# Decoding of int64-packed weights: the low words' product on ScalarE and GpSimd, with four decoding steps a unit throughout

## The chip, the cores and the metric

The kernel runs on one core of a Trainium2 chip. The core's engines work in parallel, each with a queue of its own that it goes through in order: TensorE (PE; its weight loads are shown as PEld), VectorE (DVE), ScalarE (ACT), GpSimd (POOL) and SyncE (SP), which here issues DMAs. The metric is device time in microseconds (us) of one execution; a verdict compares medians of runs on the same chip.

## The reference

Block-sparse attention over q, k and v of shape (4, 8, 768, 64), followed by a gated projection. A query block of 32 rows sees the first and the last block, its neighbours, and three drawn blocks; the first and the last query block see everything. Cut to what matters:

```python
mask = np.abs(blk_i - blk_j) <= 1
mask = mask | (blk_i == 0) | (blk_j == 0) | (blk_i == n_blocks - 1) | (blk_j == n_blocks - 1)
for qb in range(n_blocks):
    for kb in sampled_blocks[qb]:
        mask[qb * block:(qb + 1) * block, kb * block:(kb + 1) * block] = True
scores = np.where(mask, scale * np.matmul(q, k.transpose(0, 1, 3, 2)), -1e9)
attn = np.exp(scores - max); attn = attn / (sum + 1e-09)
x = (attn @ v) as (B, S, H * D)                  # 4 x 768 x 512
gate_pre = sum over k < 5 of conv_w[k] * xp[:, k:k + S]   # causal convolution
gate = 1.0 / (1.0 + np.exp(-gate_pre))
out = (gate * (x @ w_val) @ w_out)               # w_val, w_out: 512 x 512
```

The three weight arrays reach the program as float64, seen as pairs of 32-bit words: the kernel has to make float32 values of them itself.

## The kernel before

Attention goes in *units*. Each batch has eleven pairs of query blocks, one unit each, and one pair of global blocks (first and last), which takes two units: 13 units a batch, 52 in all. A main loop over steps `n` (line 684) writes the program so that each step holds, for TensorE, the scores of unit n (`sc`, or `s` for a global one), the product with the values of unit n - 2 (`av`) and the transposes of unit n - 1 (`pt`). Around that, VectorE reduces the scores to their maximum (`mx`, two instructions for a pair), then divides `av` of unit n - 2 by its sum (`rs`, `x`), which TensorE transposes (`xp`) into `xT`. ScalarE makes the exponentials (`pe`), copies the transposed probabilities to SBUF (`ptr`), `xp` to `xT`, and scales queries (`qc`). GpSimd gathers value rows (`vb`, two indirect DMAs a unit, line 343) and copies key blocks into a tile that unit n + 2 will use (`kg`, five copies, line 308). Each step's gather needs the `vb` buffer that `av` of three units earlier has read. SP loads queries, keys, end and own value rows (`va`), and weights.

The order on each engine is the order in which the program is written: `InOrder` (line 71) ties each instruction to the one before it on its engine. What belongs to no unit is dealt out in small portions, `prepare(steps)` (line 646), called twice in the step of a pair, behind each half of the transposes (line 732). A portion is one `yield` of a generator. While weights are not all decoded, a portion is a step of `decode_weights` (line 204), which runs up to two tiles in turn; afterwards it is a step of the gates' convolution (`th`, on VectorE and ScalarE). `STEPS, MORE` (line 53) give two steps a call, and three in the units listed in `MORE`.

`decode(hi, lo, raw, n)` (line 154) turns a tile of 128 x 512 float64 values into two float32 parts: `hi`, the value rounded to float32r, and `lo`, the rest. `raw` is a staging tile (`wst`) of word pairs; `hw` is the high word and `lw` the low word of each, so consecutive elements of one of them lie 8 bytes apart. `t` (`words`) is scratch. Before the change a tile takes eight steps with VectorE instructions in seven of them alone and in the eighth with ScalarE's cast of `hi`. It is called for eight tiles, four of `w_val` (into `wv0`, `wv1`) and four of `w_out` (into `wo0`, `wo1`), and for the convolution's 20 columns (`cst` into `cwp`, then `cw`). The first portions run in step 2. There are four staging tiles, so the load of a `w_out` tile on SP (line 184) waits until the `w_val` tile in the same buffer is decoded. When all are decoded, the gates start, and later the projections (`vp`, `op`) of `project` (line 548), on TensorE between the parts of the units.

Of the kernel before, what the change touches and what calls it, by code (L numbers as in the profile page):

```python
# [7 lines left out]
F32 = mybir.dt.float32  # L8
# [3 lines left out]
AF = mybir.ActivationFunctionType  # L12
ALU = mybir.AluOpType
# [36 lines left out]
    {0: POOL, 1: POOL, 2: POOL, 3: DVE, 4: ACT},  # L50
] + [{0: POOL, 1: POOL, 2: POOL}] * (B - 2)

STEPS, MORE = 2, (*range(2, 7), *range(48, 53))

HELD = ()

# [2 lines left out]
def attention_moe(ctx, tc, qb, kb, v, sampled, w_val, conv_w, w_out, ident_in, slot_in, out):  # L59
# [29 lines left out]
    pe, dve, act, pool, sp = (InOrder(e) for e in (nc.tensor, nc.vector, nc.scalar, nc.gpsimd, nc.sync))  # L89
# [42 lines left out]
    for r in range(NR):  # L132
# [3 lines left out]
            out=base[rows, :], in0=sf[rows, r, :], scalar1=float(BLK), scalar2=off[rows], op0=ALU.mult, op1=ALU.add  # L136
# [17 lines left out]
    def decode(hi, lo, raw, n):  # L154

        hw, lw = raw[:, :, 1], raw[:, :, 0]
        t = two.tile([128, DM], F32, tag="ot", name="words").bitcast(I32)[:, 0:n]
        dve.tensor_scalar(out=t, in0=hw, scalar1=0x1FF, scalar2=15, op0=ALU.bitwise_and, op1=ALU.logical_shift_left)
        yield True
        dve.scalar_tensor_tensor(  # L160
            out=lw.bitcast(U32), in0=lw.bitcast(U32), scalar=17, in1=t.bitcast(U32),
            op0=ALU.logical_shift_right, op1=ALU.bitwise_or,
        )
        yield True

        dve.tensor_scalar(out=t, in0=hw, scalar1=0x7FFFFFFF, scalar2=None, op0=ALU.bitwise_and)
        yield True
        dve.tensor_scalar(
            out=t.bitcast(F32), in0=t.bitcast(F32), scalar1=2.0**-15, scalar2=2.0**16, op0=ALU.max, op1=ALU.mult
        )  # L170
        yield True
        dve.tensor_scalar(out=t, in0=t, scalar1=3, scalar2=0x7FFFF000, op0=ALU.logical_shift_left, op1=ALU.bitwise_and)
        yield True
        dve.scalar_tensor_tensor(out=t, in0=hw, scalar=-(1 << 31), in1=t, op0=ALU.bitwise_and, op1=ALU.bitwise_or)
        yield True
        dve.tensor_scalar(out=hw, in0=t, scalar1=-(1 << 23), scalar2=None, op0=ALU.bitwise_and)
        yield True
        dve.scalar_tensor_tensor(out=lo, in0=lw, scalar=2.0**-35, in1=hw.bitcast(F32), op0=ALU.mult, op1=ALU.mult)
        act.copy(hi, t.bitcast(F32))
        yield True  # L180

# [14 lines left out]
    def decode_conv():  # L196
        yield from decode(cwp[:, 0, :], cwp[:, 1, :], cst, CH * KW)
        dve.tensor_tensor(
            out=cw.rearrange("p c k -> p (c k)"), in0=cwp[:, 0, :].bitcast(F32), in1=cwp[:, 1, :].bitcast(F32),
            op=ALU.add,  # L200
        )
        yield True

    def decode_weights():

        jobs, begun = [(-1, decode_conv())], 0
        while step[0] < DECODE_LAG:
            yield False
        while jobs or begun < 2 * CH:
            n = begun  # L210
            if len(jobs) < 2 and n < 2 * CH and len(staged) > n and step[0] >= staged[n][0] + DECODE_LAG:
                dst = wv if n < CH else wo
                jobs.append((n, decode(dst[0][:, n % CH, :], dst[1][:, n % CH, :], staged[n][1], DM)))
                begun += 1
            if not jobs:
                yield False
                continue
            n, job = jobs.pop(0)
            if next(job, None):
                jobs.append((n, job))  # L220
                yield True
            else:
                decoded.add(n)
        decoded.add("all")
# [580 lines left out]
```

## Time and profile before

| | us |
|---|---|
| three runs | 398.83, 401.76, 400.08; median 400.08 |
| profiled execution | 400.6 |
| its span, first to last instruction | 398.8 |

| engine | busy us | share of the span |
|---|---|---|
| PE | 349.5 | 88% |
| PEld | 271.4 | 68% |
| DVE | 284.3 | 71% |
| ACT | 251.7 | 63% |
| POOL | 237.9 | 60% |

In the trace a row names the engine, the operation, the tile that is written and those that are read (`words<-wst`), the shape, a count, the busy time, and in square brackets the idle time in front of it with what ended it. Stretches of the same operation are merged into one row with their count. All instructions have line 77, the helper's line, so they are told apart by their tiles. A share over the whole span mixes stages: weights are decoded from 24 to 104 us, gates run from 103 us on, and projections from 130 us on.

### The profile page before, as it was taken

The numbers are of one execution on the slowest core, as the hardware profiler recorded it, in microseconds if no ns is written. First come the engines' busy times: TensorE is split into PE (matmuls) and PEld (weight loads), VectorE is DVE, ScalarE is ACT, GpSimd is POOL, SyncE is SP. The second block draws the span as 40 slices with busy tenths as digits, with TensorE's granted clock in tenths as the row PEclk, the third lists the DMA queues.
The fourth block names the chain that finished last, engine by engine and source line by source line (L and its number), as shares of the span: only waits on it lengthen the run. The fifth ranks groups of instructions, "written<-read, shape, count | busy, mean of one in ns | idle before, by whom it ended". The sixth has DMA issues, their size and how long they took to land.

```text
span 398.8 us, 16126 instructions
## 1 busy us (share of the span) xinstructions
PE 349.5 (88%) x6616; PEld 271.4 (68%) x6616; DVE 284.3 (71%) x595; ACT 251.7 (63%) x610; POOL 237.9 (60%) x377
## 2 busy tenths in 40 slices
PE   7697777787686999899789988998999999999896
PEld 5364455565464887697568866776678788789694
DVE  4478999995889679677937783776495746957820
ACT  1487787883897776665555764666576565754521
POOL 1836887495599667726671777367537765522730
PEclk9999999998999999989999999999999999999999
DMA  7968897888756756874253557564633254120102
GB/s 246 329 190 254 286 300 231 227 241 255 226 165 201 225 160 171 257 213 138 55 181 105 148 167 214 160 206 134 201 109 103 62 149 109 53 79 26 54 26 80
DMA packets 41305, 67.15 MB, mean 168 GB/s; under 512 B 5648, under 2 KB 21904, under 8 KB 41232
## 3 DMA queue, kind: packets, MB, share of 16 engines
q1 hardware_dynamic: 34048, 42.67, 34.7%
q0 software_dynamic: 7040, 23.43, 20.9%
q8 instruction: 52, 0.85, 0.8%
q14 instruction: 21, 0.17, 0.1%
q10 hardware_dynamic: 144, 0.03, 0.1%
HBM read 59.81 MB, written 6.29 MB: 166 GB/s over the span
## 4 chain that ended last, share of the span: by engine, by line
PE 57%; DVE 19%; DMA 8%; ACT 7%; issue 6%; another core or an unknown queue 1%; POOL 1%; SPq 1%; ACTq 0%; DVEq 0%
PE op L77 15%; PE vp L77 14%; PE av L77 10%; PE pt L77 8%; PE sc L77 7%; DVE mx L77 7%; DVE words L77 4%; DMA va<-in_v 3%; DMA wst<-in_w_val 3%; DVE wst L77 2%; DVE th L77 2%; PE xp L77 2%; DMA k<-in_k 2%; PE s L77 1%; ACT ptr L77 1%
## 5 line engine op out<-in xcount | busy, mean ns | idle before, releaser
L77 POOL DMA_INDIRECT vb<-in_v,idx x88 | 89.2, 1013 | 56.6 <-PE av L77 29.6
L77 ACT ACTIVATE pe<-sc,mx 128x256 f32<-128x256 f32 x176 | 69.2, 477 | 63.4 <-DVE mx L77 59.8
L77 DVE SCALAR_TENSOR_TENSOR th<-xT,cw,th 128x384 f32<-128x384 f32 x128 | 97.8, 767 | 6.4 <-ACT th L77 3.6
L77 DVE TENSOR_REDUCE mx<-sc 128x2 f32<-128x512 f32 x88 | 56.6, 683 | 53.3 <-PE sc L77 35.2
L77 POOL COPY kg<-k 128x128 f32 (+1 forms) x220 | 78.3, 398 | 7.8 <-DMA k<-in_k 7.6
L77 POOL TENSOR_TENSOR yl<-y,yh 128x384 fp32r<-128x384 f32 x32 | 35.5, 1109 | 67.3 <-ACT yh L77 67.3
L77 ACT COPY ptr<-pt 128x512 f32<-128x512 f32 x112 | 66.0, 602 | 12.2 <-PE pt L77 7.3
L77 PE MATMUL vp<-xh,wv 128*128 128x384 f32 x256 | 72.6, 348 | 0.7 <-DVE y L77 0.7
L77 PE MATMUL av<-va,ptr 128*32 128x65 f32 x1408 | 51.4, 225 | 7.1 <-issue 6.2
L77 PE MATMUL op<-wo,yh 128*128 128x512 f32 x192 | 54.7, 410 | 0.8 <-ACT yh L77 0.6
L77 PE MATMUL pt<-ident,pe 128*128 128x128 f32 x352 | 53.9, 286 | 1.0 <-issue 1.0
L77 PEld LDWEIGHTS av<-va,ptr 128*32 128x32 f32 x1408 | 35.1, 110 | 27.3 <-issue 16.3
L77 PE MATMUL av<-vb,ptr 128*32 128x65 f32 x1408 | 49.4, 222 | 4.4 <-issue 4.2
L77 PE MATMUL sc<-kg,qc 64*32 64x256 f32 x1408 | 49.3, 388 | 0.0
L77 PEld LDWEIGHTS vp<-xh,wv 128*128 128x128 f32 x256 | 47.4, 190 | 1.3 <-DVE y L77 0.9
L77 POOL TENSOR_TENSOR xl<-xT,xh 128x384 fp32r<-128x384 f32 x32 | 35.2, 1105 | 18.8 <-ACT xh L77 17.0
L77 PEld LDWEIGHTS pt<-ident,pe 128*128 128x128 f32 x352 | 40.4, 144 | 7.8 <-issue 1.4
L77 PE MATMUL vp<-xl,wv 128*128 128x384 f32 x128 | 43.4, 339 | 0.0
L77 PEld LDWEIGHTS av<-vb,ptr 128*32 128x32 f32 x1408 | 36.8, 111 | 7.7 <-issue 7.3
L77 PEld LDWEIGHTS op<-wo,yh 128*128 128x128 f32 x192 | 33.3, 189 | 7.0 <-ACT yh L77 1.8
L77 PE MATMUL xp<-ident,x 128*128 128x128 f32 x96 | 18.9, 278 | 16.9 <-DVE x L77 8.4
L77 PEld LDWEIGHTS sc<-kg,qc 64*32 64x32 f32 x1408 | 22.2, 107 | 13.0 <-issue 6.8
(75 smaller groups left out, 473.8 us busy)
## 6 DMA issues: line engine op xcount, KB each, us to landing
va<-in_v SPq DMA_DIRECT2D x60, 130.0 KB
qc<-in_q SPq DMA_DIRECT2D x48, 128.0 KB
out<-ot SPq DMA_DIRECT2D x24, 256.0 KB
kg<-in_k SPq DMA_DIRECT2D x77, 64.0 KB
vn<-in_v SPq DMA_DIRECT2D x18, 260.0 KB
k<-in_k SPq DMA_DIRECT2D x18, 256.0 KB
wst<-in_w_val SPq DMA_DIRECT2D x4, 512.0 KB
wst<-in_w_out SPq DMA_DIRECT2D x4, 512.0 KB
```

Source lines behind the costliest of these rows:

```text
L77: made = getattr(self.eng, name)(*args, **kwargs)
```

## The change

Three things change. The last product of the decoding, `lo = lw * 2**-35 * hw`, was one VectorE instruction; now ScalarE writes `lw * 2**-35` as float32 over the low words, as soon as they are assembled, and GpSimd multiplies that with the high words. The step that held the product is joined with the one before it, so a tile takes seven steps. And the five units 2 to 6 have two steps a call, as the others do, and no longer three.

```diff
-STEPS, MORE = 2, (*range(2, 7), *range(48, 53))
+STEPS, MORE = 2, range(48, 53)
...
             out=lw.bitcast(U32), in0=lw.bitcast(U32), scalar=17, in1=t.bitcast(U32),
             op0=ALU.logical_shift_right, op1=ALU.bitwise_or,
         )
+        act.activation(lw.bitcast(F32), lw, AF.Copy, scale=2.0**-35)
         yield True
...
         dve.tensor_scalar(out=hw, in0=t, scalar1=-(1 << 23), scalar2=None, op0=ALU.bitwise_and)
-        yield True
-        dve.scalar_tensor_tensor(out=lo, in0=lw, scalar=2.0**-35, in1=hw.bitcast(F32), op0=ALU.mult, op1=ALU.mult)
+        pool.tensor_tensor(out=lo, in0=lw.bitcast(F32), in1=hw.bitcast(F32), op=ALU.mult)
         act.copy(hi, t.bitcast(F32))
         yield True
```

VectorE before, in one of the units with six steps (the one whose reductions stand at 37.25 us in the trace); names carry the number of the buffer's use, `wst_242` and `wst_339` are the first two `w_val` tiles:

```order
L77 TENSOR_REDUCE mx_752<-sc_734 128x2
L77 TENSOR_REDUCE mx_752<-sc_735 128x2
L77 TENSOR_SCALAR rs_816<-av_783 128x4
L77 RECIPROCAL rs_816<-rs_816 128x4
L77 TENSOR_TENSOR x_819<-av_783,rs_816 128x256
L77 TENSOR_SCALAR wst_242<-words_586 128x512
L77 TENSOR_SCALAR words_707<-words_707 128x512
L77 SCALAR_TENSOR_TENSOR wv1_124<-wst_242 128x512
L77 TENSOR_SCALAR words_707<-words_707 128x512
L77 SCALAR_TENSOR_TENSOR words_707<-wst_339,words_707 128x512
L77 TENSOR_SCALAR words_841<-wst_473 128x512
```

VectorE after, in the same unit:

```order
L77 TENSOR_REDUCE mx_748<-sc_730 128x2
L77 TENSOR_REDUCE mx_748<-sc_731 128x2
L77 TENSOR_SCALAR rs_812<-av_779 128x4
L77 RECIPROCAL rs_812<-rs_812 128x4
L77 TENSOR_TENSOR x_815<-av_779,rs_812 128x256
L77 TENSOR_SCALAR words_585<-words_585 128x512
L77 TENSOR_SCALAR words_825<-wst_339 128x512
L77 SCALAR_TENSOR_TENSOR words_585<-wst_242,words_585 128x512
L77 SCALAR_TENSOR_TENSOR wst_339<-wst_339,words_825 128x512
```

Between the normalisation and the next reductions stand four decoding instructions instead of six, and the product `wv1<-wst` is gone; the first tile is not yet finished here.

GpSimd before, between the key copies of one unit and those of the next (`[waits ...]` names the engines or DMA queues whose semaphores the instruction waits for):

```order
L77 COPY kg2_117<-k_133 128x128 [waits Pool_49]
L77 DMA vb_973<-in_v,idx_114 128x520 [waits DMASW5_49,DMASW4_49,PE_49]
L77 DMA vb_973<-in_v,idx_114 128x520
L77 COPY kg3_118<-k_133 128x256 [waits Pool_49]
L77 COPY kg3_118<-k_133 128x2x128 [waits Pool_49]
```

GpSimd after, at the same place:

```order
L77 COPY kg2_117<-k_133 128x128 [waits Pool_49]
L77 TENSOR_TENSOR wv1_124<-wst_242 128x512 [waits DMAHW3_49,DVE_49,Activation_49]
L77 DMA vb_966<-in_v,idx_114 128x520 [waits DMASW5_49,DMASW4_49,PE_49]
L77 DMA vb_966<-in_v,idx_114 128x520
L77 COPY kg3_118<-k_133 128x256 [waits Pool_49]
```

The product stands behind a unit's copies and in front of the next unit's gathers, and waits for VectorE and ScalarE; there are eight such places.

ScalarE after, in a unit in the middle of the decoding (`ptr` are the copies of transposed probabilities, `xT` the copy of the attention's output, `wv0` the cast of a `hi` part):

```order
L77 COPY ptr_1303<-pt_1298 128x512 [waits PE_49,Activation_49]
L77 ACTIVATE wst_607<-wst_607 128x512 [waits DMAHW4_49,DVE_49]
L77 COPY ptr_1313<-pt_1308 128x512 [waits PE_49,Activation_49]
L77 CAST wv0_123<-words_956 128x512
L77 COPY xT_597<-xp_1319 128x4x64 [waits PE_49]
```

The scaling of the low words is new; it waits for VectorE, with the second `ptr` copy and `xT` behind it. In half of the tiles it stands behind the second `ptr` copy instead. TensorE's order does not change. On SP the loads of the `w_out` tiles keep their order among themselves, and each waits for GpSimd's product where it waited for VectorE's.

## The prediction

> **What bounds the kernel now.** I read the table of stages first, then the chain of waits, then the timelines of VectorE and GpSimd in the stage in which weights are decoded. Columns of the table: stretch and its length, then busy us (and instructions) of PE, PEld, DVE, ACT and POOL, the granted clock, the DMA share and GB/s.
>
> ```profile
> 33.20:90.20 57.00, 42.51 (x1204) 29.72 (x1205) 55.82 (x118) 45.60 (x129) 44.72 (x72) 1.00 0.88 258
> 108.00:130.00 22.00, 17.01 (x516) 12.34 (x522) 19.55 (x39) 19.05 (x51) 18.59 (x31) 1.00 0.58 171
> 130.00:250.00 120.00, 112.12 (x2040) 89.49 (x2021) 85.10 (x161) 74.80 (x177) 72.42 (x119) 0.99 0.59 170
> ```
>
> From 33 to 90 us VectorE is busy for 55.82 of 57.00 us and TensorE for 42.51; from 130 us TensorE is busy for 112.12 of 120. So VectorE sets the early pace and TensorE the late one. The chain of waits says the same of the decoding stage (start, length, what):
>
> ```profile
> 51.05 1.17 DVE wst L77
> 52.22 1.13 DVE words L77 x2
> 53.34 1.19 DVE mx L77 x2
> ...
> 56.15 0.81 DVE wv L77
> 56.96 1.01 DVE words L77
> 57.97 1.19 DVE mx L77 x2
> ```
>
> `wv` is the product that the change takes away; it lies on the chain. TensorE's order is the same before and after, so what is won or lost by 130 us reaches the end nearly whole. The length of a unit is the distance between its pairs of reductions (start, length, engine, instruction, count); the first, the second and the eleventh of the stage, and TensorE's first projection from the chain:
>
> ```profile
> 37.25 1.27 DVE L77 TENSOR_REDUCE mx<-sc 128x2 f32<-128x512 f32 x2
> ...
> 42.86 1.28 DVE L77 TENSOR_REDUCE mx<-sc 128x2 f32<-128x512 f32 x2
> ...
> 86.10 1.27 DVE L77 TENSOR_REDUCE mx<-sc 128x2 f32<-128x512 f32 x2
> ...
> 132.30 2.12 PE vp L77 x12
> ```
>
> A unit with six decoding steps takes 42.86 - 37.25 = 5.6 us, the ten units take (86.10 - 37.25)/10 = 4.9 in the mean.
>
> **Term 1: eight products leave VectorE.** The two groups of products, and the two of GpSimd and the one of ScalarE that are nearest to what replaces them:
>
> ```profile
> L77 DVE SCALAR_TENSOR_TENSOR wo<-wst 128x512 fp32r<-128x512 int32 x4 | 3.2, 800 | 0.1
> L77 DVE SCALAR_TENSOR_TENSOR wv<-wst 128x512 fp32r<-128x512 int32 x4 | 3.1, 779 | 0.0
> L77 POOL TENSOR_TENSOR yl<-y,yh 128x384 fp32r<-128x384 f32 x32 | 35.5, 1109 | 67.3 <-ACT yh L77 67.3
> L77 ACT CAST wv<-words 128x512 fp32r<-128x512 f32 x4 | 2.5, 626 | 0.0
> ```
>
> The rows give 3.1 + 3.2 = 6.3 us for the eight. The step counts change with them: a tile takes seven steps instead of eight, the five units 2 to 6 take four steps instead of six, and decoding ends in the same unit (the first of batch 1's two global ones) as before, so there is no other VectorE work in the sum. The saving is the products alone, and it comes in the first units. A product that nobody disturbs costs less:
>
> ```profile
> 75.12 0.42 DVE L77 TENSOR_SCALAR wst<-words 128x512 int32<-128x512 int32 x1
> 75.45 0.42 DVE L77 TENSOR_SCALAR words<-words 128x512 f32<-128x512 f32 x1
> 75.78 0.69 DVE L77 SCALAR_TENSOR_TENSOR wo<-wst 128x512 fp32r<-128x512 int32 x1
> 76.39 0.42 DVE L77 TENSOR_SCALAR words<-words 128x512 int32<-128x512 int32 x1
> ```
>
> From 75.78 to 76.39 it holds the engine for 0.61 us, and 8 x 0.61 = 4.9. Ends: 4.9 and 6.3. I take 6.3, because in this stage nearly all of them run disturbed.
>
> **Term 2: eight products arrive on GpSimd, and slow VectorE.** GpSimd took 1.109 us for 384 elements; 512 take at most 1.109 x 512/384 = 1.48 us if all of it grows with the elements, and 8 x 1.48 = 11.8 us. (The new inputs lie 8 bytes apart, which no GpSimd row here shows; I add nothing for it.) What GpSimd's work does to VectorE is seen where the two overlap, here with copies of key blocks:
>
> ```profile
> 48.46 1.28 DVE L77 TENSOR_REDUCE mx<-sc 128x2 f32<-128x512 f32 x2
> 49.66 0.15 DVE L77 TENSOR_SCALAR rs<-av 128x4 f32<-128x4 f32 x1
> 49.85 0.18 DVE L77 RECIPROCAL rs<-rs 128x4 f32<-128x4 f32 x1
> 50.06 0.42 DVE L77 TENSOR_TENSOR x<-av,rs 128x256 f32<-128x256 f32 x1
> 50.40 0.65 DVE L77 TENSOR_SCALAR words<-words 128x512 int32<-128x512 int32 x1
> 50.97 1.25 DVE L77 SCALAR_TENSOR_TENSOR wst<-wst,words 128x512 uint32<-128x512 uint32 x1
> 52.14 0.77 DVE L77 SCALAR_TENSOR_TENSOR words<-wst,words 128x512 int32<-128x512 int32 x1
> 52.83 0.51 DVE L77 TENSOR_SCALAR words<-wst 128x512 int32<-128x512 int32 x1
> ...
> 50.65 2.83 POOL L77 COPY kg<-k 128x256 f32<-128x256 f32 x5
> ...
> 65.31 1.80 DVE L77 TENSOR_SCALAR words<-wst 128x512 int32<-128x512 int32 x1
> ...
> 65.39 1.45 POOL L77 COPY kg<-k 128x256 f32<-128x256 f32 x5
> ```
>
> Against the undisturbed 0.42 and 0.69 the four instructions took 0.65 + 1.25 + 0.77 + 0.51 = 3.18 instead of 2.22 us: 0.96 us lost to five copies that need 1.45 us when they go first, or 0.66 us a us. Always met by decoding, the products would cost 0.66 x 11.8 = 7.8 us; met by the reductions and the normalisation, which stand at 48.46 to 50.40 beside GpSimd and aren't longer than elsewhere, none. Ends: 0 and 7.8. By the order a product stands behind the copies of its unit, so it falls about as often on the next unit's reductions and normalisation (1.9 of 4.9 us, from 48.46 to 50.40) as on decoding. I take half, +3.9.
>
> The row at 65.31 is the sharp form of this: one instruction of 0.42 us lasted 1.80, all the time of the five copies. The Trainium skill (SBUF — State Buffer, § Who interferes with whom) states that VectorE and GpSimd share one pair of ports, and that whichever starts first holds it for its whole instruction while the other is blocked; the trace agrees at 65.31, while at 50.97 both sides were stretched. Taken so for all eight products, term 2 would be 11.8 and not 3.9.
>
> **Term 3: what the new places queue up.** GpSimd's product waits for ScalarE's scaled low words and VectorE's last high word of its unit, and the gathers of value rows (`vb`) of the next unit wait behind it.
>
> ```profile
> POOL vb L77 <- PE av L77: 16.5, 7, 8.5
> POOL vb L77 <- issue: 3.7, 13, 0.3
> POOL vb L77 <- PE pt L77: 0.3, 2, 0.2
> ...
> 78.10 0.97 POOL L77 DMA_INDIRECT vb<-in_v,idx  x1 [5.25 <-PE av L77]
> 79.37 1.44 POOL L77 DMA_INDIRECT vb<-in_v,idx  x1 [0.30 <-issue]
> ...
> 86.36 0.14 PEld L77 LDWEIGHTS av<-vb,ptr 128*32 128x32 f32 x6 [0.25 <-DMA vb<-in_v,idx]
> ```
>
> GpSimd waited for `av` 16.5 us up to 90 us, 8.5 of it before 33 us; so 8.0 of the 57.0 us were free, and 49.0 are its work. Six of the eight products fall there: 49.0 + 6 x 1.48 = 57.9, against VectorE's 57.0 - 6.3 + 3.9 = 54.6. GpSimd will be 3.3 us behind at the end of the stage. Gathers and copies are issued two units ahead (some 9.8 us at 4.9 a unit), and a gather that was issued by 80.81 (79.37 + 1.44) held the weight load up at 86.36 by 0.25 us, so landing took 5.5: a lead of about 4 us covers 3.3. If that cover is gone, all 3.3 us come onto the path. Ends: 0 and 3.3; I take +0.4, since only at the start of batch 1, where a gather waits for new indices, was the lead used up.
>
> ScalarE gets eight scalings more, 8 x 0.626 = 5.0 us by the cast's row, and is at 45.60 of 57.00 now: 50.6 of 54.6 fits, and what it waits for is VectorE, as the group of exponentials from 33 to 90 us shows:
>
> ```profile
> L77 ACT ACTIVATE pe<-sc,mx 128x256 f32<-128x256 f32 x46 | 18.1, 476 | 11.1 <-DVE mx L77 8.9 <-DVE words L77 2.2
> ```
>
>  The scalings stand ahead of half of the probability copies or of the `xT` copy, so one may be late by 0.6 us where VectorE makes the low words last; the next reductions (1.19 us in the chain) cover that. 0.
>
> On SP the four `w_out` loads now wait for GpSimd's product, with query and value loads behind them, which are needed two units later: 0. The gates begin half a unit later, with three instructions instead of four behind the second global unit: VectorE is busy for 19.55 of 22.00 us there, and the one instruction comes back later in the same stage: 0. The conv weights' products are 20 columns wide: 0.
>
> **Sum.** -6.3 + 3.9 + 0.4 = -2.0. The profiled execution took 400.6 us (span 398.8), so 398.6; the median of the three runs, 400.08, lies 0.5 below the profiled one, so 398.1 for the median.
>
> **Rivals.**
> - *All of it is won.* GpSimd's products fall into reductions and its lag stays inside the lead: 400.08 - 6.3 = 393.8, or 395.2 with 4.9. For it: decoding fills only some 3 of 4.9 us of a unit. Against: the copies, in the same place of the queue, now stretch every unit.
> - *VectorE is blocked for each product's whole length.* The place is the decoding behind the last high word, which wakes GpSimd and goes on with the next tile: 400.08 - 6.3 + 11.8 = 405.6, slower. It decides where over 6.3/11.8 = 53% of the products' time is lost by VectorE; the copies above reach 66%, within decoding. For it the row at 65.31; against it the reductions. The Trainium skill (SBUF — State Buffer, same section) has this as its rule.
> - *GpSimd becomes the bound.* Gathers land late, TensorE waits for `vb` as at 86.36. The stage would last 57.9 instead of 57.0, and the last two products (3.0 us) would hold up gathers as well: 400.08 + 0.9 + 3.0 = 404.0 at worst, 401 if only the stage counts.
>
> **Chances.** My sum 0.50 (own range 396 to 400.5; 0.05 of it lies below 396.1), full gain 0.22 (0.02 of it within 1%), blocking 0.15 (0.02 within), GpSimd's bound 0.13 (0.09 within, 0.04 slower). A measurement of this kernel tells some 1% from no change, 396.1 and 404.1. Faster by over 1%: 0.05 + 0.20 = 0.25; slower: 0.13 + 0.04 = 0.17; within: 0.58. The range goes from 393.6, just past the full gain, to 404.8, which holds GpSimd's bound and some of the blocking (about 0.08 above, 0.06 below left out).
>
> **What would show it.** Right: VectorE's early units of about 4.4 us instead of 5.6 (two steps of some 0.6 us fewer), eight fewer products, `mx` still at the end of a busy VectorE in most units, TensorE's first projection about 2 us earlier than 132.30. Term 2: `words` and `wst` rows longer in the mean than now, where a GpSimd `wv` or `wo` product runs beside them; those products at 1.3 to 1.5 us. Term 3: waits of TensorE's `av` for `vb`, or of `sc` for GpSimd's `kg`, of under 1 us in all. Wrong: products on GpSimd of 2 us and more (the 8-byte step), `av` waits of several us, or reductions that wait for ScalarE.

## The result, and the profile after

The kernel after is slower: 414.28 us (409.6 to 418.4, four runs) against 399.45 us for the kernel before on the same chip, a ratio of 1.032 (95% interval 1.022 to 1.043). The ratios, here and below, leave out runs more than 1.5% above the fastest of the same kernel, such as the one of 418.4 us. The forecast was 398.1 us, with a range that ended at 404.8. The profiled execution took 415.05 us, span 413.1.

The stages that the prediction showed, after (same columns):

```profile
33.20:90.20 57.00, 44.30 (x1066) 30.18 (x1064) 41.41 (x99) 44.38 (x123) 39.13 (x71) 0.94 0.78 236
108.00:130.00 22.00, 16.13 (x308) 10.86 (x308) 14.55 (x33) 13.09 (x31) 12.91 (x24) 0.77 0.43 123
130.00:250.00 120.00, 110.53 (x2139) 87.03 (x2141) 87.02 (x170) 79.10 (x190) 75.32 (x123) 0.99 0.58 166
```

VectorE is busy for 41.41 us instead of 55.82. Yet TensorE gets through 1066 matmuls where it got through 1204, and from 108 us on through 308 instead of 516. Every engine now has idle time, so something makes them wait for each other. The late stage is as it was. The granted clock of 0.77 from 108 to 130 us is not the reason: when the kernel after was run again (below), it was 1.00 in that stretch, and the loss was the same. One row dates the loss: ScalarE's copy of batch 1's global output, the only `xT` copy "x2" in this stretch, before and after.

```profile
120.52 0.47 ACT L77 COPY xT<-xp 128x128 f32<-128x128 f32 x2
```

```profile
136.48 0.46 ACT L77 COPY xT<-xp 128x128 f32<-128x128 f32 x2
```

The kernel after is 16.0 us behind there, and the spans differ by 14.3 us at the end: so the loss is there by then. The first projection in its chain of waits, which was at 132.30 us before:

```profile
147.84 2.13 PE vp L77 x12
```

GpSimd's groups from 28 to 130 us show what the new product does there (busy us, mean ns of one, then its engine's idle time in front of it and what ended it):

```profile
L77 POOL TENSOR_TENSOR wv<-wst 128x512 fp32r<-128x512 f32 x4 | 4.4, 1091 | 8.2 <-DVE wst L77 2.9 <-ACT pe L77 2.9 <-issue 2.4
L77 POOL TENSOR_TENSOR wo<-wst 128x512 fp32r<-128x512 f32 x4 | 4.3, 1064 | 9.6 <-issue 7.7 <-ACT wo L77 2.0
```

The products are short, 1.09 and 1.06 us. But GpSimd stands idle for 8.2 + 9.6 = 17.8 us in front of the eight, with the next gathers behind them in its queue. There is a ninth such place that I had not counted: the product of the convolution's 20 columns waits 9.9 us, and ends at 34.21 us. GpSimd's waits for `av` in front of its gathers from 28 to 130 us (total us, times, longest), before and after, show where the new waits went:

```profile
POOL vb L77 <- PE av L77: 20.0, 9, 8.5
```

```profile
POOL vb L77 <- PE av L77: 4.3, 2, 4.0
```

Before, GpSimd was often early and stood ready for its next gather; now it comes late. What a late gather meets, in the timeline of GpSimd and TensorE after:

```profile
44.25 1.09 POOL L77 TENSOR_TENSOR wv<-wst 128x512 fp32r<-128x512 f32 x1 [1.23 <-ACT pe L77]
...
45.50 1.02 POOL L77 DMA_INDIRECT vb<-in_v,idx  x1 [0.15 <-issue]
45.63 0.32 PE L77 MATMUL av<-va,ptr 128*32 128x65 f32 x8
...
46.81 0.30 PE L77 MATMUL av<-va,ptr 128*32 128x65 f32 x3 [0.39 <-issue]
46.82 0.95 POOL L77 DMA_INDIRECT vb<-in_v,idx  x1 [0.30 <-issue]
47.60 0.26 PE L77 MATMUL av<-va,ptr 128*32 128x65 f32 x2 [0.49 <-issue]
...
48.33 0.27 PE L77 MATMUL av<-va,ptr 128*32 128x65 f32 x2 [0.46 <-issue]
```

The gather starts when TensorE begins `av`, not behind it. Beside the two gathers, and once just behind them, TensorE goes on in small groups of matmuls, with gaps of 0.4 to 0.5 us that no semaphore explains ("issue"). The waits of `av` for "issue" from 28 to 130 us (total us, times, longest), before and after:

```profile
PEld av L77 <- issue: 5.0, 11, 0.6
PE av L77 <- issue: 2.2, 6, 0.4
```

```profile
PEld av L77 <- issue: 18.9, 37, 0.8
PE av L77 <- issue: 10.5, 25, 0.5
```

The product also meets VectorE, in the same profile:

```profile
44.48 1.15 DVE L77 TENSOR_SCALAR words<-words 128x512 f32<-128x512 f32 x1
...
62.34 1.28 DVE L77 TENSOR_REDUCE mx<-sc 128x2 f32<-128x512 f32 x2
...
85.99 2.28 DVE L77 TENSOR_SCALAR words<-wst 128x512 int32<-128x512 int32 x1 [0.31 <-ACT wo L77]
```

A decoding instruction that takes 0.42 us undisturbed lasts 1.15 us beside the product at 44.25, and 2.28 us beside five key copies and the product at 86.95; both end 0.29 us behind the product. The reductions beside the product at 62.22 are as long as before.

The theory for the experiments is therefore: *the product is a wait in GpSimd's queue, and the gathers behind it are the price* (queue theory). Its rivals: the fewer steps of units 2 to 6, the product's work and ports, and ScalarE's scalings or the joined steps.

### The profile page after: what moved, and what is told of

Same layout as the page of the kernel before. It is cut to its first block, busy times and chain, and to the rows that moved or that the text cites. A ratio compares the mean times of both kernels' runs of the same rounds, so it can differ in the third digit from the quotient of the medians.

```text
span 413.1 us, 16151 instructions
## 1 busy us (share of the span) xinstructions
PE 361.0 (87%) x6616; PEld 277.6 (67%) x6616; DVE 273.6 (66%) x586; ACT 258.2 (63%) x619; POOL 239.9 (58%) x386
## 4 chain that ended last, share of the span: by engine, by line
PE 67%; DVE 14%; issue 7%; ACT 5%; DMA 3%; another core or an unknown queue 3%; POOL 1%; DVEq 0%; SPq 0%; ACTq 0%
PE op L77 15%; PE av L77 14%; PE vp L77 14%; PE sc L77 10%; PE pt L77 10%; DVE mx L77 5%; DVE th L77 3%; PE xp L77 2%; PE s L77 2%; DMA k<-in_k 2%; DVE words L77 1%; DVE x L77 1%; DMA cst<-in_conv_w 1%; ACT ptr L77 1%
## 5 line engine op out<-in xcount | busy, mean ns | idle before, releaser
L77 POOL DMA_INDIRECT vb<-in_v,idx x88 | 88.3, 1004 | 45.8 <-PE av L77 17.1
L77 DVE SCALAR_TENSOR_TENSOR th<-xT,cw,th 128x384 f32<-128x384 f32 x128 | 98.8, 786 | 15.4 <-ACT th L77 11.7
L77 POOL COPY kg<-k 128x128 f32 (+1 forms) x220 | 70.9, 365 | 8.1 <-DVE vm L77 6.0
L77 PE MATMUL av<-va,ptr 128*32 128x65 f32 x1408 | 55.3, 227 | 12.9 <-issue 11.5
L77 PEld LDWEIGHTS av<-va,ptr 128*32 128x32 f32 x1408 | 37.2, 111 | 36.0 <-issue 25.9
L77 PE MATMUL av<-vb,ptr 128*32 128x65 f32 x1408 | 52.5, 224 | 5.9 <-issue 5.5
L77 PE MATMUL op<-wo,yh 128*128 128x512 f32 x192 | 56.1, 418 | 0.5 <-ACT yh L77 0.5
L77 PE MATMUL sc<-kg,qc 64*32 64x256 f32 x1408 | 51.0, 395 | 0.0
L77 POOL TENSOR_TENSOR xl<-xT,xh 128x384 fp32r<-128x384 f32 x32 | 36.9, 1157 | 17.5 <-ACT xh L77 15.7
L77 PEld LDWEIGHTS av<-vb,ptr 128*32 128x32 f32 x1408 | 38.5, 111 | 8.8 <-issue 8.6
```

What stands on the lines that cost most here:

```text
L77: made = getattr(self.eng, name)(*args, **kwargs)
```

## Experiments

A ratio is to the kernel before on the same chip, with its 95% interval.

**One part alone, or undone.** The steps alone, in the kernel before:

```diff
-STEPS, MORE = 2, (*range(2, 7), *range(48, 53))
+STEPS, MORE = 2, range(48, 53)
```

> The kernel before with four decoding steps a unit from the first, nothing else: all products stay on VectorE, eight steps a tile, so decoding ends some units later. Queue theory (GpSimd's product is a wait that pushes the gathers of value rows into TensorE's av, which then gets its instructions in bursts): no product on GpSimd, so gathers start behind av as before and the time stays at 397 to 404 us. Steps theory (the loss comes from fewer steps in units 2 to 6): 410 us or more. GpSimd-work theory (the product's work slows VectorE and GpSimd): as the queue theory, 397 to 404.

403.54 us, 1.009 (1.005 to 1.013). Small: the "x2" copy comes at 119.72 us, no later than before, but decoding ends late, and projections start at 148.7 us instead of 132.0. From 33.2 to 90.2 us VectorE is busy for 45.37 us with all its products, so most of the way from 55.82 to 41.41 is the slower pace. Next the opposite, the move with the six steps of before (the line above undone in the kernel after):

> The kernel after with six steps in units 2 to 6 as before: only the product's move and the joined step are left of the change. Queue theory: the GpSimd product still waits ahead of the gathers, 407 to 416 us. Steps theory: back to 395 to 402 us. GpSimd-work theory: 407 to 416, as the queue theory.

416.51 us, 1.047 (1.039 to 1.055): no better than the whole change, rather worse. The steps theory falls. Fewer steps seem to make the move cheaper. The bursts in `av` do not follow the loss here: its waits for "issue" from 28 to 130 us are 5.8 us, against 10.5 in the kernel after.

Now the wait with next to no work: the kernel before, with one GpSimd instruction of 128 x 1 a tile (`mark` is a scratch column).

```diff
         dve.tensor_scalar(out=hw, in0=t, scalar1=-(1 << 23), scalar2=None, op0=ALU.bitwise_and)
+        pool.tensor_tensor(out=mark, in0=lw[:, 0:1].bitcast(F32), in1=hw[:, 0:1].bitcast(F32), op=ALU.mult)
```

> The kernel before with one GpSimd product of 128 x 1 more a tile, of the high words when they are masked, at the place where the change puts the whole product: the wait in GpSimd's queue without its work, and without anything taken from VectorE. Queue theory: gathers start in the next unit's av as in the kernel after, with gaps of 0.4 to 0.5 us between bursts of matmuls, and the time rises to 404 to 412 us. GpSimd-work theory (1.09 us of work a product, and the ports): 399 to 402, since eight waits of work that is nearly nothing cost nothing. Steps theory: 399 to 402.

408.37 us, 1.026 (1.018 to 1.033). Its GpSimd groups:

```profile
L77 POOL TENSOR_TENSOR mark<-wst 128x1 f32<-128x1 f32 x8 | 2.9, 357 | 17.1 <-issue 17.1
```

Eight instructions of 0.36 us that stand idle for 17.1 us (and a ninth for the convolution, 6.9 us, at the start) cost 9 us, while VectorE keeps all its work. So a wait at this place is enough for a loss; it is 2.6% of the 4.7% that the move costs at the same six steps. Then the work without the wait: the kernel after, with each product written one unit later, behind that unit's gathers and copies.

```diff
-        pool.tensor_tensor(out=lo, in0=lw.bitcast(F32), in1=hw.bitcast(F32), op=ALU.mult)
+        late.append((lo, lw.bitcast(F32), hw.bitcast(F32)))
...
         until("copied", n + COPY_AHEAD, copy_keys)
+        products()
...
```

> The kernel after with each GpSimd product written one unit later, behind that unit's gathers and key copies, and a tile counted as decoded only then: the same work on every engine, but what the product waits for is done long before, so that no gather stands behind a wait. Gates begin a unit later. Queue theory: the waits ahead of GpSimd's wv and wo products (17.8 us in the kernel after) fall under 4, the gathers start behind av again, and the time falls to 393 to 401 us. GpSimd-work theory: the work is the same, so 408 us or more. Steps theory: 408 or more.

403.78 us, 1.014 (1.007 to 1.020): 3 us above the range that I gave, which had forgotten the price of the steps. GpSimd's groups and the `xT` copy:

```profile
L77 POOL TENSOR_TENSOR wo<-wst 128x512 fp32r<-128x512 f32 x4 | 4.1, 1037 | 0.0
L77 POOL TENSOR_TENSOR wv<-wst 128x512 fp32r<-128x512 f32 x4 | 4.1, 1030 | 0.0
```

```profile
120.24 0.46 ACT L77 COPY xT<-xp 128x128 f32<-128x128 f32 x2
```

The 17.8 us of waiting are 0.0 (the convolution's product still waits 9.9 us), and the copy that came at 136.48 us comes at 120.24, earlier than in the kernel before. The time is that of the steps alone (403.54): with four steps, the products on GpSimd, ScalarE's scalings, the joined step and eight fewer products on VectorE come to nothing together; whether a cost and a gain cancel in it is not shown. The place also spares VectorE: beside the late products stand mostly its reductions and normalisation, which are not stretched. So this run takes away two things at once, the wait and the stretching, and it is the 128 x 1 instruction above that shows the wait's price by itself.

The product as a plain VectorE product, with ScalarE's scaling, the joined step and four steps kept:

```diff
-        pool.tensor_tensor(out=lo, in0=lw.bitcast(F32), in1=hw.bitcast(F32), op=ALU.mult)
+        dve.tensor_tensor(out=lo, in0=lw.bitcast(F32), in1=hw.bitcast(F32), op=ALU.mult)
```

> The kernel after with the product as a plain VectorE product (ScalarE's scaling, seven steps a tile, four steps a unit all stay); GpSimd gets nothing. Queue theory: no wait in GpSimd's queue, gathers behind av, 398 to 404 us, like the steps alone (1.009 of before). If ScalarE's scaling or the joined steps were the loss: 409 us or more.

385.09 us, 1.017 (1.006 to 1.027). The kernel before took 379.01 us in this set of runs. It keeps to one of two levels within a set: 399 to 401 us in four sets, 379 in two, and one chip gave both; the expectations written below as "a chip with stalls" and "without" are to be read as these levels. On the ratio the steps alone explain this run within the intervals. Against scalings and joined steps as the loss the late product says more, since it keeps both and has the time of the steps alone.

**Without gathers.** In the kernel before, and then in the kernel after, each gather is replaced by a load of consecutive rows. The drawn rows are left out, so these kernels do not compute the attention and serve for their times alone:

```diff
-            pool.indirect_dma_start(
-                out=pr.vb[:, j, :], out_offset=None, in_=v,
-                in_offset=bass.IndirectOffsetOnAxis(ap=idx[:, b, i : i + 1], axis=0),
-            )
+            sp.dma_start(pr.vb[:, j, :], v[b * S + i * BLK // 2 : b * S + i * BLK // 2 + 128, :])
```

> The kernel before with the gathers of drawn value rows left out: 128 consecutive value rows are loaded by SP into the same buffers instead, so the bytes stay and GpSimd makes no gather. It is the base for the next run. Queue theory with stalls in av by gathers: up to 7 us less than before, for the 17 gathers that stand beside av from 130 to 360 us with TensorE busy 70% of that time, so 392 to 399 us. If a gather does nothing to av: 397 to 401.

> The kernel after with the same replacement: GpSimd's product waits as before, but no gather stands behind it, only key copies. Queue theory with stalls in av: the loss of 13 us against the base of this pair nearly goes; 390 to 400 us, at most 4 above the run before it. If the loss comes from the product's work, ScalarE's scalings, or from key copies that come late: 10 us or more above the run before it.

377.12 us, 0.996 (0.993 to 0.999), and 377.29 us, 0.995 (0.991 to 0.999), both at the 379 level and below all that I had expected, which reckoned with a base of 399 us. The pair again, at the other level, beside the kernel after:

> The kernel after, unchanged, beside the pair without gathers. The last four runs were on a chip on which the kernel before takes 379 us and gathers beside av leave TensorE busy all the time (11.5 of 11.5 us), against 399 us and 70% on the chips before. Queue theory with av stalls as the whole price: 1.03 of before on a chip with such stalls, 0.99 to 1.01 on one without. If lateness itself is the price (gathers and copies that come late, whatever av does): 1.03 on both.

> The kernel before with 128 consecutive value rows loaded by SP in place of each gather, as before (run again beside the kernel after, on the same chip). On a chip with av stalls: 0.95 to 0.98 of before, since the gathers that stand beside av no longer break it up. On one without: 0.996 again.

> The kernel after with the same replacement, on the same chip. Queue theory: the same time as the run before it within 1%, on either kind of chip. If key copies or the product's own work are the price: 10 us above it.

The kernel after took 412.04 us, 1.034 (1.026 to 1.043); the pair 376.83 us, 0.943 (0.934 to 0.952), and 377.53 us, 0.944 (0.938 to 0.950), so the first was a little faster than expected, and the two agree within 1%. This settles the main point: the product still stands in GpSimd's queue, with the key copies behind it, and the eight wait even longer (43.5 us from 28 to 130 us), but without gathers the change costs nothing. So the loss needs the gathers. GpSimd is also relieved of the gathers' own time here and comes earlier to everything, so this pair alone doesn't clear the copies; but from 28 to 130 us TensorE's scores wait 0.2 us in all for GpSimd, in the kernel after as in the kernel before. A second point: without gathers the kernel takes 377 us at both levels, so the 20 us between the levels belong to the gathers too. The waits of `av` for "issue" from 130 to 360 us, in the kernel before (first trace), without gathers, and with gathers at the 379 level (the late product with six steps, below); in the last two PE has no such wait, only PEld:

```profile
PEld av L77 <- issue: 22.7, 48, 0.6
...
PE av L77 <- issue: 9.4, 23, 0.5
```

```profile
PEld av L77 <- issue: 9.2, 23, 0.4
```

```profile
PEld av L77 <- issue: 9.4, 23, 0.6
```

At the 379 level this gather does not break `av` up; a piece of that kernel's timeline, beside which the one at 45.50 above is to be held:

```profile
191.93 0.95 POOL L77 DMA_INDIRECT vb<-in_v,idx  x1 [0.31 <-issue]
...
192.03 0.30 PE L77 MATMUL av<-va,ptr 128*32 128x65 f32 x8
192.14 0.30 PE L77 MATMUL av<-vb,ptr 128*32 128x65 f32 x8
192.25 0.30 PE L77 MATMUL av<-va,ptr 128*32 128x65 f32 x8
192.37 0.30 PE L77 MATMUL av<-vb,ptr 128*32 128x65 f32 x8
```

What becomes of VectorE's 6.3 us shows in the pair, too. ScalarE's `xT` copy of batch 0's seventh pair, without gathers, before and after (second set):

```profile
66.68 0.39 ACT L77 COPY xT<-xp 128x256 f32<-128x256 f32 x1
```

```profile
63.81 0.38 ACT L77 COPY xT<-xp 128x256 f32<-128x256 f32 x1
```

Here the change is 2.9 us ahead, the most at any `xT` copy of the stage. Two units later, at 74.75 us, the lead is 1.1: in front of `pt` TensorE waits 2.96 us for "issue" where it waits 1.59 without the change. The rest goes at the next wait for value rows (TensorE's timeline of the kernel after without gathers; without the change the wait is 2.78 us), and the "x2" copy comes at 119.79 us, against 119.61:

```profile
90.94 0.32 PE L77 MATMUL av<-vb,ptr 128*32 128x65 f32 x8 [3.79 <-DMA vb<-in_v]
```

**The late product with six steps**, the best guess for a faster kernel (the first diff of this part undone in the late product):

> The late product (GpSimd's product one unit later, behind that unit's gathers and copies) with six steps in units 2 to 6 as in the kernel before. Queue theory with the price of the steps (0.9%) on top: what was left of the loss goes, VectorE is relieved of its eight products and decoding ends earlier than before, so 393 to 400 us. If the late product still costs by its work or its ports: 402 to 408, as with four steps or above.

> The late product with six steps in units 2 to 6, which took 1.034 of before on the chip without av stalls. If what it loses is a loss of its own (its traces there show TensorE 134 matmuls behind by 53 us, at a granted clock of 0.82): 1.03 again on any chip. If its loss came from that chip or that run: 1.00 to 1.015, as the late product with four steps.

391.46 us, 1.034 (1.023 to 1.044), at the 379 level, and 407.03 us, 1.020 (1.013 to 1.026), at the other: a miss both times. Six steps with tiles of seven cost time of their own, and at the 379 level without stalls of `av`. With six steps the parts add up: the wait alone 1.026, the late product 1.020, and the move with its wait 1.047; with four steps it is 1.014 without the wait and 1.032 with it. So the wait costs 1.8 to 2.7% in each of the three pairs, and at six steps something else in the move costs 2.0%. By the "x2" copy (123.28 us, against 119.35 without gathers) about 4 of its 12 us at the 379 level had been lost. What this cost is I did not find.

**A late gather elsewhere.** The kernel before, with the gathers of steps 26 to 49 behind a GpSimd copy that waits for that step's maxima; the kernel before beside it took 399.91 us (399.22 in the run that was traced):

```diff
...
+            if not un.pr.glob:
+                pool.tensor_copy(mark, un.mx[:, 1, 0:1])
+            gather_now(held.pop(0))
...
```

> The kernel before with the gathers of steps 26 to 49 written behind that step's scores, behind a GpSimd copy of one column of mx: they start when the unit's maxima are there, which is when TensorE begins av. No product is moved, decoding is untouched, and the new copy has one column. av-stall theory: nearly all of these some 36 gathers now stand beside av, where 17 of 44 stood before; with matmuls of av at some 22 a us beside a gather on the slow-gather chips and 51 on the other chip, each more costs some 0.55 us, so 10 us for 19 more: 1.02 to 1.035 of before on a chip with stalls, 0.995 to 1.01 on one without. Lateness theory (data or copies late, whatever av does): TensorE waits for DMA of vb, not for issue, on any chip; if neither counts here, 1.00.

> The kernel before, for its trace on this chip: 400 us where gathers beside av leave TensorE busy 70% of their time, 379 us where they leave it busy all the time.

408.08 us, 1.021 (1.016 to 1.025). The number is the one I gave, the reason is not. TensorE's waits from 130 to 360 us, then the base's:

```profile
PE op L77 <- POOL yl L77: 10.9, 4, 6.3
...
PE av L77 <- issue: 4.2, 10, 0.4
```

```profile
PE av L77 <- issue: 9.6, 23, 0.5
```

The gathers came so late that they missed `av`, whose waits for "issue" fell to less than half. The loss came from `op`, which waits for GpSimd's `yl` behind the new wait. So this run shows that a wait in GpSimd's queue can cost through other work behind it as well, and not what a broken `av` costs.

**The same rows without gathers.** A gather's 128 rows are four blocks of 32 rows, so SP can load them at row numbers from registers: all (in the kernel before and after), half from batch 1 on, and all from batch 2 on.

```diff
+            sp.dma_start(pr.vb[0:BLK, j, :], v[r0 : r0 + BLK, :])
...
+            for r, reg in enumerate(regs):
+                sp.dma_start(pr.vb[BLK * (r + 1) : BLK * (r + 2), j, :], v[bass.ds(reg, BLK), :])
```

> The kernel before with every gather replaced by plain loads on SP that fetch the same rows: a slot of 32 rows is one block, so eight DMAs of 32 rows a pair, six of them at a row number read from SBUF into a register; 31 more rows of zeros stand behind v for the slots that are masked. GpSimd makes no gather. If the gathers are the price, as the runs without them showed: 376 to 384 us, on any chip, so 0.94 to 0.96 of before where that takes 400 and about 1.00 where it takes 379. If SP's six register loads and eight DMAs a unit become late: TensorE waits for vb's DMA, 390 us or more.

> The same replacement in the kernel after. If the loss of the change came through the gathers alone: within 1% of the run before it. If moving the product has a gain of its own once nothing waits behind it: up to 6 us less than the run before it (the eight products that left VectorE). If the product's wait also costs through the key copies behind it: 3 us more or worse.

> The kernel before with the second of a unit's two gathers replaced, from batch 1 on, by four SP loads of 32 rows at row numbers held in registers (the same rows; 31 more rows of zeros behind v). SP is busy 47% in the late stage now; one register load of 0.70 us, three DMAs at 0.25 and one at 0.55 add about 2 us to a unit of 6.8, so 0.77. Gathers as the price: a third to a half of the 23 us that the kernel without gathers won, so 387 to 394 us where before takes 400. SP as the bound: 402 us or more, with waits of TensorE for vb's DMA.

> The kernel before with both gathers of a unit replaced in the same way, from batch 2 on only, with one register load a unit instead of two. SP's added work is some 3.7 us of a unit of 6.8 on top of 3.2: at the edge. Gathers as the price: 384 to 391 us where before takes 400. SP as the bound: 402 us or more, with waits of TensorE for vb's DMA and SP busy all the time from 130 us on.

501.41 us (1.255, 1.249 to 1.260) and 501.32 us (1.256, 1.250 to 1.261) where before took 399.91; 397.59 us (1.049, 1.044 to 1.054) and 422.14 us (1.111, 1.106 to 1.116) where before took 379.35. The gain that I looked for came in none. In the first and the last SP as the bound, the other branch, holds; the second says nothing of the change, since SP bounds it too; the third lies between its two branches. SP's queue, and TensorE's waits from 130 us on, in the first of them:

```profile
250.79 6.05 SPq L77 DMA_DIRECT2D vb<-in_v  x8
...
260.70 4.27 SPq L77 DMA_DIRECT2D vb<-in_v  x5
```

```profile
PE av L77 <- DMA vb<-in_v: 35.8, 20, 3.7
```

Eight loads, with the register loads between them, hold SP for 6.05 us of a unit, and TensorE waits for their data. With half of them that wait is 4.1 us from 130 us on, with all from batch 2 on 16.4. These runs put SP's cost in the place of the gathers'; no version that loads the drawn rows beats the kernel before.

## Why the prediction was wrong

- *Term 3, GpSimd's queue (+0.4, ends 0 and 3.3): this step failed.* I added GpSimd's busy times (57.9 against 54.6 us) and called a lead of 4 us a cover. The product's own waiting was not in that sum: 17.8 us in the profile after, in a queue whose 8.0 free us from 33 to 90 us I had seen as room. That room was GpSimd standing ready for its next gather (`vb <- PE av`, 20.0 us from 28 to 130 us, and 4.3 after); the wait consumed it and pushed the gathers on. The wait alone costs 1.026, and with the product out of the way 1.032 falls to 1.014. The convolution's product I had put at 0 by its width of 20 columns; it too is a wait, of 9.9 us, but the late product keeps it, so it is no part of what the late product wins back.
- *The price of a late gather.* I priced it as data that land late, from the 0.25 us at 86.36. Up to 130 us the lateness of the data is not what the waits name. It is the start itself: beside a gather `av` runs in bursts, and its waits for "issue" rise from 2.2 to 10.5 us. The trace of before had such rows in its late stage, 9.4 us of them, and I hadn't looked there. That these bursts make up the 14 us is not shown, and the move alone speaks against it, with more loss and only 5.8 us of such waits; that the loss needs the gathers is shown.
- *Term 1, -6.3.* The saving on VectorE is there, the gain isn't: with four steps a unit the time is the same with the products on VectorE (403.54) and off it (403.78). With four steps VectorE is no longer the bound, at 45.37 of 57.00 us with all its products. But with six steps the late product loses 2.0%, so the pace isn't the whole reason, and the rest is open. Without gathers the change was ahead by 2.9 us at most, and TensorE's next waits took it.
- *Term 2, +3.9 for VectorE slowed by GpSimd.* The mechanism is there: decoding instructions beside a product were held until it ended (1.15 us instead of 0.42 at 44.48, 2.28 at 85.99), and reductions were not, as I had read. What it costs in time is not shown: with four steps VectorE has slack. The products took 1.06 to 1.09 us, below the bound of 1.48. The rival that VectorE is blocked for each product's whole length (405.6), which the Trainium skill (SBUF — State Buffer, § Who interferes with whom) has as its rule for VectorE instructions that use the shared ports, was near in sign and wrong in cause: a wait that leaves VectorE its work costs 2.6%. The rows at 44.48 and 85.99 agree with that rule in the blocking. Of who goes first the row at 65.31, which I cited for it, says the opposite: VectorE's row starts 0.08 us ahead of the copies, and yet it is the one that was held.
- *Four steps a unit at no cost.* Alone they cost 1.009: decoding ends later, and projections with it. The steps and the wait make 0.9% and 2.6%, about the 3.2% measured; that two terms meet it so closely is partly luck, since with six steps, where the pace is as before, the move costs 4.7%.
- *GpSimd as the bound (401 to 404).* The engine was right, the mechanism wrong: not a busy engine, a waiting one.
- *What would show it.* `av` waits of several us came, as named for being wrong, but for "issue"; waits for `vb` and `kg` stayed under 1 us, which I had named as a sign of being right. The first projection came 15.5 us later, not 2 us earlier; the steps alone delay it as much, at a third of the loss, so it doesn't point to the queue.

Open: by which path late gathers cost their time, the bursts in `av` or another; what the move costs besides the wait at six steps; what the change costs at the 379 level, where the kernel after was not run and `av` shows no such bursts (the late product with six steps loses 3.4% there); and why a session has one level or the other.

## What to carry to other kernels

Before work is moved to an engine with spare time, ask what it waits for and what is queued behind it: in an in-order queue a wait can be a price by itself, without any work, and an engine's idle time may be its readiness for a transfer that others need. Place such work behind the urgent instructions of the next round, where its inputs are long done; here that brought the waits from 17.8 us to 0.0 and the loss from 3.2% to 1.4%. And a busy share of 98% is no promise that relieving the engine wins: here it won nothing, neither with four steps a unit, which take VectorE off the bound anyhow, nor with six.

## What the runs showed of the hardware that was not expected

A gather on GpSimd can slow TensorE, which does not need its rows until two units later: at the 400 level `av`, many small matmuls with a weight load each, goes beside gathers in groups with gaps of 0.4 to 0.5 us. Take the gathers from 130 to 360 us beside which at least ten `av` matmuls ran: in the kernel before there were 231 such matmuls in 13.3 us of gathers, in the late product with six steps at the 379 level 526 in 12.7 us. The Trainium skill (Perfetto Trace Analysis, § DMA Instruction — SWDGE (GPSIMD)) says that the row of such a DMA ends when its last descriptor is written, not when the data have moved. By that rule gaps beside the rows at 45.50 and 46.82 would go with the writing of descriptors; but the gap before 48.33 begins behind the end of the second row (47.77 us), and no run here separates the writing from the moving.

The kernel before has two levels on the same chip, 379 and 400 us, and without gathers it has one (376.8 and 377.1 us). And loads at row numbers from registers were dear for the queue that issues them: eight loads, six of them such, held SP for 6.05 us with their register loads, where the two plain loads behind them take 0.37 and 0.42 us. The Trainium skill (Perfetto Trace Analysis, § DMA Optimizations) says that spreading DMAs over the engines that can issue them may help when descriptor generation is the bottleneck; here the engine that took them over became the bottleneck.
